# Attention times v for two heads at once into four common PSUM banks, float64 weights converted in pairs of blocks, and a table of shifted due times

## The chip, the cores and the metric

The kernel runs on one core of a Trainium2 chip. Its metric is the time of one execution on the device in microseconds; the median of three runs stands for a kernel. A profile is one further execution, with its own time.

## The reference

Three parts follow one another, on 4 batches, 8 heads, 576 positions and heads of 64 (2304 tokens of width 512):

```
scores = q @ k^T / 8                       # per batch and head, 576 x 576
mask   = scores >= 32nd largest of its row
attn   = softmax(scores where mask, else -1e9)
x = (attn @ v), heads side by side         # 2304 x 512
h = x @ w_in;  g = h * sigmoid(1.702 h);  x = g @ w_out     # 512 -> 2048 -> 512
a = x @ w1;  b = x @ w2;  out = ((a * b) @ w3) @ w_out2     # 512 -> 1024 -> 1024 -> 512
```

q, k and v are float32. The six weight matrices come as float64 (37.7 MB in all). In the kernel moe2's w_out is called w4.

## The kernel before, in words

**Tiles.** The 2304 tokens are 18 tiles of 128. For each tile the kernel runs eight heads (`head`), then `tile_end` (the attention output is scaled and split), then `moe` (both feed-forward parts). A number that must be more exact than float16 is held as a high and a low float16 half, so each product of 512 x 512 x 128 is four blocks of three matmuls, 12 in all (`product_op`, lines 532 to 534). A tile needs 168 such matmuls: four products `h` with w_in, four steps of `x2` with w_out, two each of `a` and `b` with w1 and w2, and two steps of `o` with w34, which is w3 times w4, worked out once.

**A head.** `S` (line 760) writes the scores into one of two double PSUM banks. VectorE finds the 32nd largest by four MAX8 and three MATCH_REPLACE8 (lines 782 and 785). ScalarE cuts, takes the exponential and makes the high half (lines 800, 803, 809), GpSimd the low half (812, 813). A DMA transpose of SyncE's queue (`f_t`, line 816) brings both into one of the two buffers `ats`. Nine matmuls (`f_av`, line 823) multiply by v. The sums of two heads lie side by side in the one PSUM bank `av_ps`; ScalarE copies one half of them into `xsb` (`x0`, line 863) and VectorE adds the other (`x1`, line 867). The products have three PSUM banks of their own (`mm`).

**The weights.** `load64` turns a float64 block of 128 x 512 into float32 without reading it as a number: a load into a raw buffer (line 372), then `w low` (ScalarE, line 377), `w sign` (ScalarE line 387 or GpSimd line 382), `w main` (ScalarE, line 391) and `w join` (VectorE, line 395), which frees the raw buffer. The 72 blocks go through in the order w4, w3, w_in, w_out, w1 and w2. Raw buffers are borrowed: eight in the place of w12 for w4 and w3 (`raw_c`), four in the place of wout for w_in and w_out (`raw_b`), and two for w1 and w2 (`raw_t`), one of which is the tile `psb` and one a part of `tsb`. Each converted block adds to a Gram matrix (line 422), from which its matrix's scale comes; then an fp32 matmul by the identity (line 459) and two instructions (lines 462 and 465) split it into halves. Where one matrix's float32 blocks lie, the next matrix's halves are put later, so the matrices follow each other.

**The order.** Nothing is scheduled by the compiler. `Order.run` simulates the five engines (T for TensorE, V, A, G and D for SyncE's DMA queue) with a cost per operation, takes for each free engine the ready operation with the smallest due time, hands out buffers of the pools, and emits the instructions in that order, in which each engine then runs them. Due times come from `head_due` (9 us apart for the first 16 heads, then 5.7), from `conv_due` (2 us for each weight block) and offsets in the code. Where an operation can go to two engines, the second has an extra wait, as `SIGN_G` for the sign on GpSimd.

Of the kernel before, what the change touches and what calls it, by code (L numbers as in the profile page):

```python
# [35 lines left out]
class Order:  # L36
# [22 lines left out]
    def op(self, alts, due, deps=(), env=None, acq=(), rel=(), tag="", lat=None):  # L59
        o = Op()  # L60
        o.alts, o.prio, o.lat = alts, due, lat
        o.acq = [(a, env, a) if isinstance(a, str) else a for a in acq]
        o.rel = [(a, env, a) if isinstance(a, str) else a for a in rel]
        o.left, o.users, o.ready, o.end, o.why = 0, [], 0.0, None, None
        o.tag, o.seq, o.done = tag, len(self.ops), False
        for d in deps:
            if d is not None:
                d.users.append(o)
                o.left += 1
        self.ops.append(o)  # L70
        return o
# [98 lines left out]
SIGN_G = 0.5  # L170
# [7 lines left out]
def kernel(  # L178
# [56 lines left out]
    def raws(w, n, first=0):  # L235
        return [w[:, (first + 2 * i) * C : (first + 2 * i + 2) * C] for i in range(n)]
# [9 lines left out]
    tsb = mem([P, 7, C], F32, "tsb")  # L246
    hsb = mem([P, 3, 2 * C], F16, "hsb")
    fsb = mem([P, 3, C], F32, "fsb")
    psb = mem([P, 2, C], F32, "psb")
# [12 lines left out]
    av_ps = ps.tile([P, C], F32, tag="av", name="av")  # L262
    m_ps = [ps.tile([P, C], F32, tag=f"mm{i}", name=f"mm{i}") for i in range(3)]
# [32 lines left out]
    od.pool("av", [av_ps[:, 0 : 2 * VW].rearrange("p (j w) -> p j w", j=2)])  # L296
# [67 lines left out]
    def load64(dst, src, raw_pool, deps):  # L364

        E = {}
        due = conv_due()

        def f_load():
            nc.sync.dma_start(E[raw_pool].bitcast(U32), src.bitcast(U32))
# [28 lines left out]
        sg = op([("A", 0.63, f_sign_a, 0.0), ("G", 0.75, f_sign, SIGN_G)], due, deps=[lo], tag="w sign")  # L401
        mn = act(0.57, due, f_main, deps=[ld, sg], tag="w main")
        return dve(0.65, due, od.two(f_join), deps=[sg, mn], env=E, rel=[raw_pool], tag="w join")
# [112 lines left out]
    def rows(w, i, j):  # L516
        return w[i * P : (i + 1) * P, j * C : (j + 1) * C]
# [27 lines left out]
    def weights():  # L545
        c4 = [load64(block(wout, i), w4[i * P : (i + 1) * P, :], "raw_c", []) for i in range(8)]
        c3 = [load64(block(win, 2 * f + kc), rows(w3, f, kc), "raw_c", []) for f in range(8) for kc in range(2)]
# [8 lines left out]
        cin = [load64(block(w12, 4 * j + i), rows(w_in, i, j), "raw_b", c3 + sp4) for j in range(NG) for i in range(KB)]  # L556
# [3 lines left out]
        for f in range(8):  # L560
# [35 lines left out]
        cout = [  # L596
            load64(block(w12, i), w_out[i * P : (i + 1) * P, :], "raw_b", cin + [ready["win"][i]]) for i in range(16)
        ]
        io, so, do = l2_scale([block(w12, i) for i in range(16)], cout)
        ready["wout"] = split_all(wout, 0, [block(w12, i) for i in range(16)], so, [do] + cout + pr, "wout")  # L600
        srcs = [rows(w, i, j) for w in (w1, w2) for j in range(NP_) for i in range(KB)]
        c12 = [load64(block(w12, i), srcs[i], "raw_t", [ready["wout"][i]]) for i in range(16)]
# [142 lines left out]

    def head(t, h, X):
# [70 lines left out]

        def f_av():
            for b, s0, r, n in pt:
                v2 = vhold[b, hp]["v2"]  # L820
                for i in range(9):
                    blk = i if i < 5 else i - 5
                    nc.tensor.matmul(  # L823
                        X["av", hp][r : r + n, j], E["at"][:, i, r : r + n], v2[:, j, blk, :], start=(i == 0), stop=(i == 8)
                    )
# [6 lines left out]
        s = pe(0.5 if len(pt) == 1 else 0.65, due - 1000 - 8, f_s, deps=qready[t] + kd, env=E, acq=["sp"], rel=rel, tag="S")  # L832
# [8 lines left out]
        for i in range(3):  # L841
# [11 lines left out]
        rel = [("v2", vhold[b, hp], "v2") for b, _, _, _ in pt if j == 1 and t == tiles_of[b][-1]]  # L853
        av = pe(
            0.55 if len(pt) == 1 else 0.75, due - 1000 + 10, f_av, deps=[tr] + vd + [X["av op", h - 1] if j else None],
            acq=[] if j else [("av", X, ("av", hp))], rel=[("at", E, "at")] + rel, tag="av",
        )
        X["S", h] = s
        X["av op", h] = av
        if j == 1:  # L860

            def f_x0():
                nc.scalar.copy(X["x"][:, 2 * hp : 2 * hp + 2, :], X["av", hp][:, :, D : P + 1])

            def f_x1():
                xs = X["x"][:, 2 * hp : 2 * hp + 2, 0:D]
                nc.vector.tensor_tensor(xs, xs, X["av", hp][:, :, 0:D], op=ALU.add)

            x0 = act(0.17, due + 12, f_x0, deps=[X["av op", h - 1], av, X.get("x0")], env=X, acq=["x"] if hp == 0 else [], tag="x0")
            X["x0"] = X["x0p", hp] = x0  # L870
            X["x1", hp] = dve(0.2, due - 40, f_x1, deps=[x0], env=X, rel=[("av", X, ("av", hp))], tag="x1")
# [68 lines left out]
    def moe(t, X):  # L940
# [8 lines left out]
        gs = []  # L949
        for j in range(NG):  # L950
# [3 lines left out]
                [X["xt"]] + ready["win"][4 * j : 4 * j + 4], [("mm", E, "mm")], [("t", X, "t")] if j == NG - 1 else [], "h",  # L954
# [20 lines left out]
            a = act(0.58, due, f_th, deps=[pr, ths], env=E, acq=["f"], tag="tanh")  # L975
            a = act(0.53, due, f_th1, deps=[a], tag="th1")
# [46 lines left out]
        ps_, pd = [], []  # L1023
        for j in range(NP_):
# [3 lines left out]
                [x2t] + ready["w12"][4 * j : 4 * j + 4], [("mm", Ea, "mm")], [], "a",  # L1028
# [120 lines left out]
```

## Time and profile before

| | |
|---|---|
| median of three runs | 1120.21 us (1118.58 to 1121.06) |
| the profiled execution | 1122.92 us, of which its span is 1121.1 us |
| busy in it: TensorE, VectorE, ScalarE, GpSimd | 987.4, 938.6, 833.6, 755.6 us |
| DMA packets' share of 16 engines | 67.6% on SyncE's queue |

The span goes from the first to the last instruction. Busy time is the union of an engine's instructions, so overlapping matmuls count once, and a stretch that is busy all through still can hold fewer matmuls than it might. A wait row names the instruction that stood still and the one that released it.

### The profile page before, as it was taken

The numbers are of one execution on the slowest core, as the hardware profiler recorded it, in microseconds if no ns is written. First come the engines' busy times: TensorE is split into PE (matmuls) and PEld (weight loads), VectorE is DVE, ScalarE is ACT, GpSimd is POOL, SyncE is SP. The second block draws the span as 40 slices with busy tenths as digits, with TensorE's granted clock in tenths as the row PEclk, the third lists the DMA queues.
The fourth block names the chain that finished last, engine by engine and source line by source line (L and its number), as shares of the span: only waits on it lengthen the run. The fifth ranks groups of instructions, "written<-read, shape, count | busy, mean of one in ns | idle before, by whom it ended". The sixth has DMA issues, their size and how long they took to land.

```text
span 1121.1 us, 18684 instructions
## 1 busy us (share of the span) xinstructions
PE 987.4 (88%) x5798; PEld 504.9 (45%) x5798; DVE 938.6 (84%) x2079; ACT 833.6 (74%) x1589; POOL 755.6 (67%) x1092
## 2 busy tenths in 40 slices
PE   1367898688879999999999998999999999999995
PEld 1233343344434445555445454454445555455442
DVE  4798899699799999989999878998998999997311
ACT  6987858988978776878788687777777777777421
POOL 6733332555547886989798887878879796776320
PEclk9998999879989999999999999999999999999998
DMA  7969958768746675786776859576865664746331
GB/s 236 293 151 229 257 101 221 197 138 177 160 113 110 128 132 118 127 167 115 136 143 122 155 103 156 107 131 124 134 140 97 135 136 94 144 83 122 76 57 38
DMA packets 428740, 156.96 MB, mean 140 GB/s; under 512 B 406624, under 2 KB 414816, under 8 KB 428640
## 3 DMA queue, kind: packets, MB, share of 16 engines
q1 hardware_dynamic: 428640, 155.78, 67.6%
q8 instruction: 45, 0.74, 0.3%
q14 instruction: 55, 0.45, 0.1%
HBM read 52.43 MB, written 4.72 MB: 51 GB/s over the span
## 4 chain that ended last, share of the span: by engine, by line
PE 38%; DVE 16%; DMA 14%; ACT 12%; POOL 12%; issue 7%; SPq 1%; POOLq 0%; ACTq 0%; DVEq 0%
PE mm L532 10%; PE mm L534 10%; PE mm L533 10%; DVE m8s L782 7%; DVE wsb L785 6%; DMA ats<-hlb 5%; DMA tsb<-hsb 5%; PE av L823 4%; PE s_ps L760 3%; POOL hsb L343 2%; POOL hlb L813 2%; ACT ysb L803 2%; POOL hsb L935 1%; ACT s_ps L800 1%; PE mm L459 1%
## 5 line engine op out<-in xcount | busy, mean ns | idle before, releaser
L782 DVE MAX8 m8s<-wsb 128x8 f32<-128x576 f32 x432 | 323.6, 755 | 5.3
L785 DVE MATCH_REPLACE8 wsb<-m8s,wsb 128x576 f32<-128x576 f32 x288 | 213.8, 743 | 0.0
L532 PE MATMUL mm<-w,tsb 128*128 128x512 f16 x432 | 164.5, 381 | 12.8 <-DMA tsb<-hsb 10.2
L532 PEld LDWEIGHTS <-tsb 128*128 128x128 f16 x1072 | 105.2, 98 | 136.9 <-DMA tsb<-hsb 28.3
L813 POOL TENSOR_TENSOR hlb<-ysb,hlb 128x512 f16<-128x512 f32 x144 | 166.7, 1158 | 0.0
L534 PE MATMUL mm<-w,tsb 128*128 128x512 f16 x432 | 164.2, 380 | 0.0
L533 PE MATMUL mm<-w,tsb 128*128 128x512 f16 x432 | 164.2, 380 | 0.0
L534 PEld LDWEIGHTS <-tsb 128*128 128x128 f16 x1072 | 105.4, 98 | 128.8 <-issue 4.0
L533 PEld LDWEIGHTS <-tsb 128*128 128x128 f16 x1072 | 105.4, 98 | 116.0 <-issue 17.1
L532 PE MATMUL mm<-wout,tsb 128*128 128x512 f16 x352 | 134.0, 381 | 7.9 <-DMA tsb<-hsb 4.0
L782 DVE MAX8 m8s<-s_ps 128x8 f32<-128x576 f32 x144 | 109.1, 757 | 34.6 <-PE s_ps L760 29.6
L800 ACT ACTIVATE s_ps<-s_ps,m8s 128x576 f32<-128x576 f32 x144 | 102.5, 712 | 44.6 <-DVE m8s L782 36.8
L534 PE MATMUL mm<-wout,tsb 128*128 128x512 f16 x352 | 133.9, 380 | 0.0
L533 PE MATMUL mm<-wout,tsb 128*128 128x512 f16 x352 | 133.9, 380 | 0.0
L803 ACT ACTIVATE ysb<-s_ps,nbs,asm 128x576 f32<-128x576 f32 x144 | 119.7, 831 | 16.9 <-DVE nbs L792 10.6
L823 PE MATMUL av<-v2s,ats 128*128 128x130 f16 (+1 forms) x1440 | 105.7, 224 | 20.2 <-DMA ats<-hlb 17.1
L532 PE MATMUL mm<-win,tsb 128*128 128x512 f16 x288 | 111.6, 388 | 9.8 <-DMA tsb<-hsb 6.2
L760 PE MATMUL s_ps<-kts,qts 128*128 128x288 f16 (+1 forms) x640 | 101.0, 298 | 18.6 <-ACT ysb L803 15.4
L823 PEld LDWEIGHTS <-ats 128*128 128x128 f16 (+1 forms) x1440 | 90.2, 102 | 57.7 <-DMA ats<-hlb 29.6
L970 POOL TENSOR_TENSOR fsb<-fsb 128x512 f32<-128x512 f32 x68 | 87.0, 1279 | 38.1 <-ACT fsb L961 37.0
L533 PE MATMUL mm<-win,tsb 128*128 128x512 f16 x288 | 111.2, 386 | 0.0
L534 PE MATMUL mm<-win,tsb 128*128 128x512 f16 x288 | 111.2, 386 | 0.0
(182 smaller groups left out, 1877.8 us busy)
## 6 DMA issues: line engine op xcount, KB each, us to landing
w<-in_moe_w_dram SPq DMA_DIRECT2D x16, 512.0 KB, 6.8
wout<-in_moe_w_in_dram SPq DMA_DIRECT2D x16, 512.0 KB, 5.2
wout<-in_moe_w_out_dram SPq DMA_DIRECT2D x16, 512.0 KB, 4.5
qts<-qts SPq DMA_DIRECT2D x36, 128.0 KB, 2.4
out_dram<-fsb SPq DMA_DIRECT2D x18, 256.0 KB, 2.5
w<-in_moe_w_out_dram SPq DMA_DIRECT2D x8, 512.0 KB, 4.6
psb<-in_moe_w_dram SPq DMA_DIRECT2D x8, 512.0 KB, 4.8
tsb<-in_moe_w_dram SPq DMA_DIRECT2D x8, 512.0 KB, 5.6
```

Source lines behind the costliest of these rows:

```text
L343: nc.gpsimd.tensor_tensor(lo(), src(), hi(), op=ALU.subtract)
L532: nc.tensor.matmul(o, a[:, i, :], hi, start=(first and i == 0), stop=False)
L533: nc.tensor.matmul(o, a[:, i, :], lo, start=False, stop=False)
L534: nc.tensor.matmul(o, a[:, 4 + i, :], hi, start=False, stop=(last and i == 3))
L760: nc.tensor.matmul(E["sp"][r : r + n, i], qe[q_][:, h, r : r + n], kt[:, j, i * HS : (i + 1) * HS], start=k_ == 0, stop=k_ == 1,)
L782: nc.vector.max(out=E["m8"][:, 8 * i : 8 * i + 8], in_=E["sp"] if i == 0 else E["w"])
L785: nc.vector.match_replace(out=two(E["w"]) if i == 0 else E["w"], in_to_replace=E["m8"][:, 8 * i : 8 * i + 8], in_values=E["sp"] if i == 0 ...
L800: nc.scalar.activation(E["sp"], E["sp"], AF.Prelu, bias=E["m8"][:, TOPK - 1 : TOPK], scale=-1.0, alpha=1.0 / FAR)
L803: nc.scalar.activation(two(E["y"]), E["sp"], AF.Exp, bias=E["nb"], scale=nesc)
L813: nc.gpsimd.tensor_tensor(hl()[:, S + SR : 2 * S], E["y"][:, 0:SM], hl()[:, 0:SM], op=ALU.subtract)
L823: nc.tensor.matmul(X["av", hp][r : r + n, j], E["at"][:, i, r : r + n], v2[:, j, blk, :], start=(i == 0), stop=(i == 8))
L970: nc.gpsimd.tensor_tensor(E["f"], E["f"], E["f2"], op=ALU.mult)
```

## The change

Attention times v is issued once for two heads, when both transposes have landed, into any one of four common `mm` banks, and both `ats` buffers come free after it. A conversion takes two blocks: a load of 1 MB, and each of the four operations over 1024 columns, with half as many raw buffers of twice the size; `raw_t` becomes one. `psb` and `tsb` become one tile. Some operations get an order among themselves (`S` after `S`, products `h`, `a` and `b` in turn, `he` after `tanh`). Every due time is shifted by an amount from a table by kind of operation and time (`LATER`, 83 kinds by 8 times), some engine choices by `LONGER`, and `SIGN_G` is 0. The diff, cut to its core:

```
-        o.alts, o.prio, o.lat = alts, due, lat
+        o.alts, o.prio, o.lat = [(e, c, f, max(w + LONGER.get((tag, e), 0.0), -1.0) if len(alts) > 1 else w) for e, c, f, w in alts], due + later(tag, due), lat
...
-SIGN_G = 0.5
+SIGN_G = 0.0
+TIMES = (-20, 60, 130, 220, 330, 500, 750, 1000)
+LATER = {
+    'S': (22, -25.5, -29.5, -19.5, -7, -8.5, -11, -16),
+    'a T': (7, 2.5, 26, 10.5, 13.5, 38, 9, 6),
+    'av': (-30, -25.5, -16, 15, 24.5, 40, 19, -0.5),
+    'gram': (7.5, 4.5, 14, 56.5, 72.5, 72.5, 69.5, 86.5),
+    'w load': (0, 3.5, -18, -0.5, 30.5, 49, -1, 2),
+    'w sign': (-1.5, 6, 0, -23, -23.5, -13.5, -12.5, -13.5),
...
+}
+LONGER = {
+    ('g hi', 'V'): 2, ('g lo', 'V'): -5.5, ('g lo', 'G'): -1.5, ('kv hi', 'V'): 7, ('kv lo', 'V'): -3.5,
...
+}
+def later(tag, due):
+    v = LATER.get(tag)
+    if v is None:
+        return 0.0
+    x = min(max(due + 1000 if due < -500 else due, TIMES[0]), TIMES[-1])
+    j = max(i for i in range(len(TIMES) - 1) if TIMES[i] <= x)
+    w = (x - TIMES[j]) / (TIMES[j + 1] - TIMES[j])
+    return v[j] * (1 - w) + v[j + 1] * w
...
-        return [w[:, (first + 2 * i) * C : (first + 2 * i + 2) * C] for i in range(n)]
+        return [w[:, (first + 4 * i) * C : (first + 4 * i + 4) * C] for i in range(n)]
...
+    tpsb = mem([P, 9, C], F32, "tpsb")
+    tsb, psb = tpsb[:, 0:7], tpsb[:, 7:9]
...
-    av_ps = ps.tile([P, C], F32, tag="av", name="av")
-    m_ps = [ps.tile([P, C], F32, tag=f"mm{i}", name=f"mm{i}") for i in range(3)]
+    m_ps = [ps.tile([P, C], F32, tag=f"mm{i}", name=f"mm{i}") for i in range(4)]
...
-        ld = dma(1.3, due - 20, f_load, deps=deps, env=E, acq=[raw_pool], tag="w load", lat=3.6)
-        lo = act(0.65, due, f_low, deps=[ld], tag="w low")
+        ld = dma(1.3, due - 20, f_load, deps=deps, env=E, acq=[raw_pool], tag="w load", lat=1.8 + 1.8 * n)
+        lo = act(0.2 + 0.44 * n, due, f_low, deps=[ld], tag="w low")
...
+    def load_pairs(w, first, srcs, raw_pool, deps):
+        res = []
+        for i, src in enumerate(srcs):
+            k_ = first + 2 * i
+            res += [load64(w[:, k_ * C : (k_ + 2) * C], src.bitcast(U32), raw_pool, deps(i))] * 2
+        return res
...
-    od.pool("raw_c", raws(w12, 8))
-    od.pool("raw_b", raws(wout, 4))
-    od.pool("raw_t", [tsb[:, 5:7, :].rearrange("p a b -> p (a b)"), psb.rearrange("p a b -> p (a b)")])
+    od.pool("raw_c", raws(w12, 4))
+    od.pool("raw_b", raws(wout, 2))
+    od.pool("raw_t", [tpsb[:, 5:9, :].rearrange("p a b -> p (a b)")])
...
         def f_av():
-            for b, s0, r, n in pt:
...
+            for j_, e in enumerate((X["E", h - 1], E)):
+                for b, s0, r, n in pt:
...
-        av = pe(
-            0.55 if len(pt) == 1 else 0.75, due - 1000 + 10, f_av, deps=[tr] + vd + [X["av op", h - 1] if j else None],
-            acq=[] if j else [("av", X, ("av", hp))], rel=[("at", E, "at")] + rel, tag="av",
-        )
...
         if j == 1:
+            av = pe(
+                1.06 if len(pt) == 1 else 1.4, due - 1000 + 10, f_av, deps=[X["tr", h - 1], tr, last_of.get("av")] + vd,
+                acq=[("mm", X, ("av", hp))], rel=[("at", X["E", h - 1], "at"), ("at", E, "at")] + rel, tag="av",
+            )
...
-                he = act(0.48, due, f_he, deps=[pr], env=E, acq=[("f", E, "f2")], rel=["mm"], tag="he")
+                he = act(0.48, due, f_he, deps=[pr, ta], env=E, acq=[("f", E, "f2")], rel=["mm"], tag="he")
```

## Rows read from the trace of the kernel before

**Rows 1.** The page's first two parts: busy time of each engine, and the busy share of the span's 40 slices in tenths (28 us each), with TensorE's granted clock.

```profile
span 1121.1 us, 18684 instructions
PE 987.4 (88%) x5798; PEld 504.9 (45%) x5798; DVE 938.6 (84%) x2079; ACT 833.6 (74%) x1589; POOL 755.6 (67%) x1092
PE   1367898688879999999999998999999999999995
...
DVE  4798899699799999989999878998998999997311
ACT  6987858988978776878788687777777777777421
...
PEclk9998999879989999999999999999999999999998
```

**Rows 2.** Busy time by stretch, over three stretches: to the last split of a weight, from there to the end of the heads, and the rest. Columns: stretch, its length, busy time (and instructions) of TensorE's matmuls, its weight loads, VectorE, ScalarE and GpSimd, then the granted clock, the DMA engines' share and GB/s.

```profile
0.00:345.00 345.00, 245.53 (x1294) 124.10 (x1295) 287.38 (x599) 286.19 (x523) 172.11 (x255) 0.94 0.79 187
345.00:1035.00 690.00, 667.78 (x4165) 347.69 (x4164) 634.30 (x1445) 522.13 (x1018) 564.62 (x813) 1.00 0.68 127
1035.00:1122.00 87.00, 74.08 (x342) 33.09 (x340) 16.93 (x36) 25.27 (x49) 18.87 (x26) 0.95 0.28 58
```

**Rows 3.** TensorE's instructions in order of time, the end of the weights' splits, a single head's attention times v between products, two heads' back to back, and a piece of the last stretch. Columns: start, time, line and operation, count.

```profile
343.01 2.14 PE L459 MATMUL mm<-w,ident 128*128 128x512 f32 x4
...
701.76 0.68 PE L823 MATMUL av<-v2s,ats 128*128 128x130 f16 x9
702.28 0.38 PE L532 MATMUL mm<-w,tsb 128*128 128x512 f16 x1
...
489.69 1.21 PE L823 MATMUL av<-v2s,ats 128*128 128x130 f16 x18
490.74 0.38 PE L532 MATMUL mm<-win,tsb 128*128 128x512 f16 x1
...
1050.03 0.38 PE L534 MATMUL mm<-wout,tsb 128*128 128x512 f16 x1
1050.25 0.38 PE L532 MATMUL mm<-wout,tsb 128*128 128x512 f16 x1
```

**Rows 4.** What TensorE waited for, in all, how often and the longest: first in the stretch to 345 us, then from 345 us to the end.

```profile
PE s_ps L760 <- ACT ysb L803: 13.1, 7, 5.0
PE mm L422 <- DVE w L395: 12.7, 7, 3.9
PE av L823 <- DMA ats<-hlb: 12.1, 8, 3.1
PE mm L422 <- DVE wout L395: 9.0, 2, 4.9
PE mm L422 <- DVE win L395: 8.8, 5, 3.2
...
PE mm L532 <- DMA tsb<-hsb: 17.1, 13, 7.1
PE av L823 <- DMA ats<-hlb: 5.0, 7, 1.3
PE mm L532 <- ACT fsb L967: 2.6, 2, 1.3
```

**Rows 5.** The sign of the conversion, line 387 on ScalarE and line 382 on GpSimd, and two casts of ScalarE of different length, as groups by form: busy time, mean ns, idle time before.

```profile
L387 ACT ACTIVATE w<-wout 128x512 f16<-128x512 f32 x19 | 14.5, 778 | 0.0
L387 ACT ACTIVATE win<-w 128x512 f16<-128x512 f32 x11 | 8.3, 769 | 0.0
L387 ACT ACTIVATE w<-psb 128x512 f16<-128x512 f32 x7 | 5.4, 770 | 0.0
L387 ACT ACTIVATE wout<-w 128x512 f16<-128x512 f32 x5 | 3.8, 764 | 0.0
L387 ACT ACTIVATE w<-tsb 128x512 f16<-128x512 f32 x6 | 4.6, 774 | 0.0
L809 ACT CAST hlb<-ysb 128x576 f16<-128x576 f32 x144 | 97.1, 677 | 5.7 <-DMA ats<-hlb 4.4
L929 ACT CAST hsb<-fsb 128x512 f16<-128x512 f32 x68 | 42.0, 618 | 13.6 <-POOL fsb L970 11.7 <-DMA tsb<-hsb 1.6
```

**Rows 6.** The instructions on the tile `psb`, one of the two raw buffers of w1 and w2, from 230 to 330 us: line, engine, operation, count, shortest, median and longest in ns, first and last start.

```profile
L372 SPq DMA_DIRECT2D psb<-in_moe_w_dram x8: 333/528/635, 233.9 to 315.0; - x8
L377 ACT ACTIVATE w<-psb x8: 763/786/796, 241.1 to 320.1; 128x512 uint16<-128x512 uint8 x8
L391 ACT ACTIVATE psb<-psb x8: 645/656/680, 243.6 to 322.6; 128x512 f32<-128x512 f32 x8
L395 DVE SCALAR_TENSOR_TENSOR w<-psb,w x8: 674/936/1420, 244.4 to 323.3; 128x512 uint32<-128x512 uint32 x8
DMA to landing us min/median/max: 3.8/4.8/5.2
```

**Rows 7.** What SyncE's queue waited for from 345 to 1035 us, the largest rows and the one on attention times v.

```profile
SPq L816 <- POOL hsb L935: 43.8, 20, 4.7
SPq L1077 <- POOL psb L342: 36.2, 14, 7.8
SPq L1077 <- ACT hsb L329: 29.4, 8, 6.3
SPq L816 <- POOL hlb L813: 26.9, 22, 3.4
...
SPq L816 <- PE av L823: 11.5, 14, 2.4
```

More of the change, by code (lines that the diff above doesn't have):

```diff
@@ L368, in load64 @@
         E = {}
-        due = conv_due()
+        n = dst.shape[1] // C
+        due = 0.0
+        for _ in range(n):
+            due = conv_due()
         def f_load():
-            nc.sync.dma_start(E[raw_pool].bitcast(U32), src.bitcast(U32))
+            raw = E[raw_pool].bitcast(U32)
+            nc.sync.dma_start(raw if n == 1 else raw.rearrange("p (n c) -> p n c", n=n), src)
         def f_low():
@@ L397, in f_join @@
             )
-        ld = dma(1.3, due - 20, f_load, deps=deps, env=E, acq=[raw_pool], tag="w load", lat=3.6)
-        lo = act(0.65, due, f_low, deps=[ld], tag="w low")
-        sg = op([("A", 0.63, f_sign_a, 0.0), ("G", 0.75, f_sign, SIGN_G)], due, deps=[lo], tag="w sign")
-        mn = act(0.57, due, f_main, deps=[ld, sg], tag="w main")
-        return dve(0.65, due, od.two(f_join), deps=[sg, mn], env=E, rel=[raw_pool], tag="w join")
+        ld = dma(1.3, due - 20, f_load, deps=deps, env=E, acq=[raw_pool], tag="w load", lat=1.8 + 1.8 * n)
+        lo = act(0.2 + 0.44 * n, due, f_low, deps=[ld], tag="w low")
+        sg = op([("A", 0.19 + 0.44 * n, f_sign_a, 0.0), ("G", 0.2 + 0.55 * n, f_sign, SIGN_G)], due, deps=[lo], tag="w sign")
+        mn = act(0.13 + 0.44 * n, due, f_main, deps=[ld, sg], tag="w main")
+        return dve(0.08 + 0.57 * n, due, od.two(f_join), deps=[sg, mn], env=E, rel=[raw_pool], tag="w join")
+    def load_pairs(w, first, srcs, raw_pool, deps):
[4 more added lines that the diff above has]
+        return res
     ncol = [0]
@@ L545, in weights @@
     def weights():
-        c4 = [load64(block(wout, i), w4[i * P : (i + 1) * P, :], "raw_c", []) for i in range(8)]
-        c3 = [load64(block(win, 2 * f + kc), rows(w3, f, kc), "raw_c", []) for f in range(8) for kc in range(2)]
+        c4 = load_pairs(wout, 0, [rows(w4, i, 0) for i in range(4)], "raw_c", lambda i: [])
+        across = [w3[f * P : (f + 1) * P, :].rearrange("p (n c) -> p n c", n=2) for f in range(8)]
+        c3 = load_pairs(win, 0, across, "raw_c", lambda i: [])
         i4, s4, d4 = l2_scale([block(wout, i) for i in range(8)], c4)
@@ L555, in weights @@
         )
-        cin = [load64(block(w12, 4 * j + i), rows(w_in, i, j), "raw_b", c3 + sp4) for j in range(NG) for i in range(KB)]
+        cin = load_pairs(w12, 0, [rows(w_in, i, j) for j in range(NG) for i in range(KB // 2)], "raw_b", lambda i: c3 + sp4)
         sp3, pr = [], []
@@ L595, in weights @@
         ready["win"] = split_all(win, 0, [block(w12, i) for i in range(16)], si, [di] + sp3, "win")
-        cout = [
-            load64(block(w12, i), w_out[i * P : (i + 1) * P, :], "raw_b", cin + [ready["win"][i]]) for i in range(16)
-        ]
+        cout = load_pairs(w12, 0, [rows(w_out, i, 0) for i in range(8)], "raw_b", lambda i: cin + ready["win"][2 * i : 2 * i + 2])
         io, so, do = l2_scale([block(w12, i) for i in range(16)], cout)
         ready["wout"] = split_all(wout, 0, [block(w12, i) for i in range(16)], so, [do] + cout + pr, "wout")
-        srcs = [rows(w, i, j) for w in (w1, w2) for j in range(NP_) for i in range(KB)]
-        c12 = [load64(block(w12, i), srcs[i], "raw_t", [ready["wout"][i]]) for i in range(16)]
+        srcs = [rows(w, i, j) for w in (w1, w2) for j in range(NP_) for i in range(KB // 2)]
+        c12 = load_pairs(w12, 0, srcs, "raw_t", lambda i: ready["wout"][2 * i : 2 * i + 2])
         ready["c12"] = c12
@@ L816, in f_t, with heads_av @@
             nc.sync.dma_start_transpose(out=E["at"], in_=hl())
+        def heads_av():
+            return X["av", hp][:, 0 : 2 * VW].rearrange("p (j w) -> p j w", j=2)
         def f_av():
-            for b, s0, r, n in pt:
[L820 to L824, printed above, removed]
-                    )
+            for j_, e in enumerate((X["E", h - 1], E)):
+                for b, s0, r, n in pt:
+                    v2 = vhold[b, hp]["v2"]
+                    for i in range(9):
+                        blk = i if i < 5 else i - 5
+                        nc.tensor.matmul(
+                            heads_av()[r : r + n, j_], e["at"][:, i, r : r + n], v2[:, j_, blk, :], start=(i == 0), stop=(i == 8)
+                        )
         kd = [d for b, _, _, _ in pt for d in kready[b, hp]]
@@ L949, in moe @@
         gs = []
+        pr = None
         for j in range(NG):
@@ L973, in f_t @@
                 nc.sync.dma_start_transpose(out=E["t"], in_=E["h"])
-            a = act(0.58, due, f_th, deps=[pr, ths], env=E, acq=["f"], tag="tanh")
-            a = act(0.53, due, f_th1, deps=[a], tag="th1")
+            ta = act(0.58, due, f_th, deps=[pr, ths], env=E, acq=["f"], tag="tanh")
+            a = act(0.53, due, f_th1, deps=[ta], tag="th1")
             if tail or (t * NG + j) % 8 < G_DVE:
@@ L1027, in moe @@
                 due + 5 * j, lambda Ea=Ea: Ea["mm"], lambda: x2e["x2t"], w12, [4 * j + i for i in range(4)], True, True,
-                [x2t] + ready["w12"][4 * j : 4 * j + 4], [("mm", Ea, "mm")], [], "a",
+                [x2t, pb] + ready["w12"][4 * j : 4 * j + 4], [("mm", Ea, "mm")], [], "a",
             )
```

38 lines of the change are left out of this document (24 added, 14 removed), and 71 rows, old and new, of tables (LATER, LONGER).

## Prediction

> **What bounds the kernel now.** I read the page's slices first. TensorE is busy 88% of the span, but not evenly: its slices stand at 6 to 9 up to about the thirteenth and at 9 from there on, while VectorE's stand at 8 and 9 nearly throughout [rows 1]. So there are stretches with different limits, and I cut the span in three. The first cut is at 345 us, where the last split of a weight ends [rows 3]; the second at 1035 us, where VectorE's work on heads ends. In the middle stretch TensorE is busy 667.78 of 690 us (97%) and VectorE 634.30 (92%): the reader should see TensorE as the bound there, with 22 us to be had at most by that measure. In the last stretch TensorE works off what is left, 74 of 87 us. In the first it is busy 245.53 of 345 us, idle 99 us, while ScalarE (286.19, 83%) and VectorE (287.38, 83%) are the busiest [rows 2].
>
> A busy TensorE isn't a TensorE that could do no more, so I check with starts. In the last stretch matmuls of 512 columns are marked 0.38 us long but start 0.22 us apart (1050.03, 1050.25), and a head's nine small ones take 702.28 - 701.76 = 0.52 us up to the next product's start [rows 3]. From 1035 us on the matmuls are dense, so the work there can't shrink by order. The consequence for the whole: after 345 us the end is TensorE's work that is left plus small stalls, so a change pays mostly through the first stretch, by having the weights ready earlier.
>
> Third, the waits. Before 345 us TensorE waits for conversions (line 422 behind the joins of line 395: 12.7 + 9.0 + 8.8 = 30.5 us), for score banks (13.1) and for the heads' transposes (12.1). After it, of its 22 + 13 idle microseconds 17.1 are for products' transposes (7.1 of them one wait), 5.0 for heads' transposes and 2.6 for a bank that ScalarE still reads (line 967) [rows 4].
>
> **The change, part by part.** *Attention times v for two heads.* Eighteen matmuls at a time. Two such groups back to back took 490.74 - 489.69 = 1.05 us, against 2 x 0.52 = 1.04 for two single ones [rows 3]. So by the nearest row the pairing gains 0, and I take that. The bound for a gain: a single group is marked 0.68 us, 0.16 more than its place; were that tail saved once for each of 72 pairs, it were 12 us. Bound for a loss: 0, for the matmuls stay the same.
>
> *Four common banks.* A bank for v was private; now a product can have it whenever no pair is in it. The only wait for a bank after 345 us that the trace shows is 2.6 us [rows 4], since an order made for three banks avoids the others. I take -5 for banks and order together in the middle stretch: about a quarter of its 22 us. Bounds: -12 (half) and +10.
>
> *Both `ats` buffers are held until the pair is done.* A third transpose must wait for the pair. One before already waited for the product at times: 11.5 us in 14 waits, 2.4 the longest [rows 7]. Between pairs of heads lie 12.3 us in the middle stretch (112 heads remain after the 32 whose work starts in the first 345 us: 690 / 112 = 6.2 each); I estimate the time needed from a landing to the freed pair at 1.05 us plus a queue of a few products, so I cost it at nothing. Its cover is that slack; without it, see the rivals.
>
> *Half as many conversions.* Of the 72 signs 48 are on ScalarE [rows 5], so it issues 36 + 36 + 24 = 96 fewer instructions (low, main, sign). The fixed part of one, from two casts: 677 ns for 576 columns and 618 for 512, so 0.92 ns a column and 618 - 472 = 146 ns that don't shrink [rows 5]. 96 x 0.146 = 14.0 us off ScalarE's 286.19: 272.2. VectorE saves 36 fixed parts, no more than a few microseconds; it isn't the sole bound there, so 0. SyncE issues 36 loads fewer of 0.53 us each [rows 6], some 19 us, on a queue whose waits are far longer; 0 too, as these waits cover it. SIGN_G at 0 can move signs from ScalarE to GpSimd, which has most of its time free before 345 us (172 of 345 busy [rows 2]); no gain or loss taken.
>
> A page bears on the fixed part: the Trainium skill, VectorE: DVE Perf Modes, section "The TRN2 errata", says that a ScalarE instruction with its source in SBUF pays 224 cycles at 1.2 GHz whatever its length, which is 187 ns; rows 5 give 146. By the page the saving would be an estimated 17.9 us instead of 14.0, and the sum some 4 us lower.
>
> *Fewer, larger raw buffers.* This speaks against the change. For w1 and w2 two raw buffers become one. Before, `psb` was loaded eight times between 233.9 and 315.0 us, one cycle in 81.1 / 7 = 11.6 us, and the other buffer goes in step with it, so two blocks take 11.6 us. Such a cycle is a load of 4.8 us, four operations of 0.786 + 0.770 + 0.656 + 0.936 = 3.15 us, and 3.65 us of waiting [rows 5, 6]. After: the load of 1 MB between 4.8 and 9.6 us, taken at 5.8, since the two loads before also shared the DMA engines; the operations 2 x 3.15 - 4 x 0.146 = 5.7; the waiting taken at half, 1.8, as part of it was for the other buffer's turn on the same engines, bounds 0.5 and 3.65. That is 13.3 us, +1.7, and over seven cycles +12 us. Bounds: 11.0 (-4 in all) and 19.0 (+52).
>
> *The tuned order.* Every due time moves, so every step may; what bounds the gain is the busiest engine of the first stretch. With ScalarE's 272.2 us at today's share, 83%, it would last 328 us; at VectorE's share of the middle stretch, 92%, 296 us. I take 88%, half-way: 309 us, -36. That is the largest choice in this working. With the raw buffers' +12 the first stretch is 24 us shorter, 321 us. Bounds: -53 (92%, and -4) and +35 (83%, and +52). In the middle stretch VectorE must keep up: its 921.7 us before 1035 would have to fit in about 1006, a share of 92%, as high as it reached there [rows 2]. The last stretch stays: 0.
>
> *Sum.* -5 - 36 + 12 = -29 us. The profiled execution took 1122.92 us (span 1121.1): 1093.9. The median of the runs shown is 2.7 below the profiled one, so 1091.
>
> **The rivals.** *One raw buffer sets the first stretch* (slower). Place: w1 and w2, from 234 to 345 us. If the load takes 9.6 and the waits stay, +52 instead of +12, and the sum is +11: 1131; if the order also only reaches 83%, -17 instead of -36, about 1150. It decides from a cycle of 11.6 + (5 + 36) / 7 = 17.5 us on. For it: the order is fixed by modelled costs, the chip adds waits, and with one buffer nothing covers a late load. Against it: TensorE can do products h and x2 of the first tiles meanwhile, and the other buffer's work no longer stands in between. For the load's price there is also a figure: the Trainium skill, DMA: Bandwidth & Descriptors, section "Bandwidth", gives 6.15 us of DMA time for 1 MB from HBM. By that the sum would be an estimated 2 us higher than with my 5.8; no trace of before has such a load.
>
> *The order gains nothing on the chip.* The transposes, not the due times, hold TensorE up, and the first stretch stays at ScalarE's 83%: 328 us, but with +12 again: -17 + 12 = -5, or 1115. For it: the waits for transposes and for loads don't shorten by a new order. Against: 30.5 us of TensorE's waits are for joins, which an order can bring forward.
>
> *The order gains more.* The first stretch at 92%, the cycle of the raw buffer unchanged, 12 us of the middle stretch and some 10 of the last (13 idle): -49 - 12 - 10 = -71, 1049; halfway between this and the forecast 1070. Against it: VectorE would need a share of 95% and more before its end.
>
> *The pair holds up SyncE's queue.* If each of the 56 pairs in the middle stretch stopped it for the 2.4 us seen at worst, that is 134 us of queue; the four largest waits there sum to 136 us [rows 7] beside TensorE's 22 us of idle time, so about 22 us would reach the end: 1113.
>
> **How the numbers follow.** The forecast, 1075 to 1105 us, has 0.43; the larger gain, below 1075, 0.19; nothing gained or the queue held up, 1105 to 1122, 0.18, of which 0.05 lies within 0.2% of before; the raw buffer and other new waits, above 1122, 0.20. A difference under 0.2%, about 2 us, can't be told from none here. So faster 0.75, same 0.05, slower 0.20. The predicted time is 1091. The range of 8 in 10 is 1057 to 1128: it leaves out the far part of the larger gain (0.08) and of the raw-buffer rival (0.12).
>
> **What would show it.** Right: the last matmul of line 459 near 320 us instead of 345; ScalarE's share before it near 88%; loads of w1 and w2 some 13 us apart; TensorE still at 97% from there, and the groups of line 823 at about 1.05 us for 18. Wrong on the raw buffer: loads 17 us or more apart and waits of line 422 above 30 us. Wrong on the order: the first stretch near 335 us. Wrong on the buffers `ats`: waits of the queue at line 816 for line 823 far above 11.5 us, and waits of TensorE for products' transposes above 17 us. The prediction fails altogether if VectorE doesn't keep up, when the heads end after 1020 us and TensorE idles before the last tile.

## The result, and where the time went

The changed kernel takes 1086.81 us (median, 1085.55 to 1087.44) against 1120.63 for before, measured beside it. The ratio is 0.9703, with a 95% interval of 0.9676 to 0.9729: 3.0% faster, 33.8 us. I had forecast 1091. The profiled execution took 1085.55 us.

Its span is 1083.4 us. First the same stretches as in [rows 2], busy time by engine, same columns:

```profile
0.00:345.00 345.00, 252.26 (x1428) 135.77 (x1430) 294.47 (x608) 280.36 (x445) 204.03 (x284) 0.91 0.79 196
345.00:1035.00 690.00, 683.88 (x4214) 357.27 (x4212) 622.66 (x1424) 525.49 (x1022) 560.51 (x797) 1.00 0.67 126
1035.00:1122.00 87.00, 37.32 (x161) 15.96 (x159) 6.75 (x14) 10.22 (x20) 7.42 (x11) 0.95 0.11 24
```

In the first 345 us TensorE is busy 7 us longer than before; in the next 690 us it is busy 16 us longer and now idle 6 of them. So the larger part of the gain is not where the prediction had it. Nor does the clock bring it: the granted clock of the first stretch is 0.91, against 0.94 before.

Busy time hides overlap, so for the rest of this document I count TensorE's work by starts: each matmul at the step from start to start in a dense run (0.2157 us for 512 columns, 0.1225 for 288, 0.058 for attention times v, 0.44 for half an fp32 block, 0.057 for a Gram piece). This is 942 to 943 us in every kernel here, since all issue the same matmuls. What a stretch has beyond its work is lost time: waits, and matmuls at a lower granted clock. It is good to some 2 us. In microseconds:

```
                                     lost to 400   400 to 950   rest   span of profile
before                                   137           25        16        1121.1
changed                                  124            1        15        1083.4
```

The spans differ by 37.7 us, the lost times by 13 + 24 + 1 = 38. That they agree proves nothing, as the lost time is the span less the same work; what the table adds is where the time was lost.

TensorE's waits from 345 us to the end answer to the second part of [rows 4]. Columns: what waited for what, us in all, times, longest.

```profile
PE mm L650 <- DMA tpsb<-hsb: 9.0, 5, 6.7
PE s_ps L879 <- ACT ysb L922: 3.2, 3, 1.6
PE mm L650 <- ACT fsb L1092: 0.8, 1, 0.8
```

Of the 9.0 us for products' transposes 6.7 are one wait; it was 17.1 us in 13 waits before. The heads' transposes don't appear any more, and the waits for a product's bank are down from 2.6 to 0.8.

The raw buffer of w1 and w2, now one for a pair of blocks, answers to [rows 6] (line, engine, operation, count, shortest, median, longest ns, first and last start):

```profile
L481 SPq DMA_DIRECT2D tpsb<-in_moe_w_dram x8: 368/380/585, 236.1 to 334.9; - x8
L486 ACT ACTIVATE w<-tpsb x8: 1349/1368/1392, 247.8 to 341.5; 128x1024 uint16<-128x1024 uint8 x8
L500 ACT ACTIVATE tpsb<-tpsb x8: 1132/1152/1179, 251.1 to 344.7; 128x1024 f32<-128x1024 f32 x8
L504 DVE SCALAR_TENSOR_TENSOR w<-tpsb,w x8: 1205/1226/2516, 252.6 to 346.7; 128x1024 uint32<-128x1024 uint32 x8
```

One cycle is (334.9 - 236.1) / 7 = 14.1 us, where two blocks took 11.6 before. The weights therefore end later, not earlier: the last matmuls of the splits stand here, and at 343 us in [rows 3].

```profile
363.17 3.70 PE L576 MATMUL mm<-w,ident 128*128 128x512 f32 x8
```

Yet by 345 us TensorE and VectorE had done more of other work. Groups by form in the first 345 us, the first MAX8 of a head and the first matmul line of the products, of the changed kernel:

```profile
L650 PE MATMUL mm<-wout,tpsb 128*128 128x512 f16 x112 | 44.6, 398 | 9.2 <-DMA tpsb<-hsb 8.3 <-DVE w L709 0.6 <-DVE hsb L582 0.4
L901 DVE MAX8 m8s<-s_ps 128x8 f32<-128x576 f32 x37 | 28.0, 756 | 6.8 <-PE s_ps L879 5.9 <-ACT hlb L928 0.7 <-ACT hsb L1053 0.2
L650 PE MATMUL mm<-win,tpsb 128*128 128x512 f16 x48 | 18.2, 379 | 0.0
L650 PE MATMUL mm<-w,tpsb 128*128 128x512 f16 x4 | 1.5, 379 | 0.0
```

and of before:

```profile
L532 PE MATMUL mm<-wout,tsb 128*128 128x512 f16 x96 | 36.9, 384 | 7.2 <-DMA tsb<-hsb 3.3 <-DVE w L590 1.8 <-ACT fsb L967 1.1
L782 DVE MAX8 m8s<-s_ps 128x8 f32<-128x576 f32 x32 | 24.2, 757 | 8.6 <-PE s_ps L760 8.5
L532 PE MATMUL mm<-win,tsb 128*128 128x512 f16 x40 | 16.4, 409 | 3.1 <-ACT fsb L967 2.0 <-DVE win L465 0.6 <-DVE hsb L1005 0.5
L532 PE MATMUL mm<-w,tsb 128*128 128x512 f16 x8 | 3.0, 379 | 0.0
```

So 164 against 144 on the first of three product lines, 60 matmuls more or 13 us of work, and 37 heads begun against 32.

### The profile page after: what moved, and what is told of

The parts are those of the page before. It is cut to its first block, busy times and chain, and to the rows that moved or that the text cites. A ratio compares the mean times of both kernels' runs of the same rounds, so it can differ in the third digit from the quotient of the medians.

```text
span 1083.4 us, 18424 instructions
## 1 busy us (share of the span) xinstructions
PE 973.5 (90%) x5798; PEld 509.0 (47%) x5798; DVE 923.9 (85%) x2045; ACT 816.1 (75%) x1485; POOL 772.0 (71%) x1091
## 4 chain that ended last, share of the span: by engine, by line
PE 52%; DVE 13%; ACT 12%; DMA 9%; POOL 6%; issue 5%; SPq 0%; DVEq 0%; ACTq 0%; POOLq 0%
PE mm L650 14%; PE mm L651 13%; PE mm L652 13%; DVE m8s L901 5%; PE mm L946 4%; DVE wsb L904 4%; PE s_ps L879 4%; DMA tpsb<-hsb 3%; PE mm L576 3%; DMA ats<-hlb 3%; DMA wout<-in_moe_w_in_dram 1%; POOL hlb L932 1%; ACT ysb L922 1%; ACT w L486 1%; DVE w L504 1%
## 5 line engine op out<-in xcount | busy, mean ns | idle before, releaser
L650 PE MATMUL mm<-w,tpsb 128*128 128x512 f16 x432 | 164.9, 382 | 8.5 <-DMA tpsb<-hsb 8.5
L650 PEld LDWEIGHTS <-tpsb 128*128 128x128 f16 x1072 | 105.3, 98 | 137.1 <-DMA tpsb<-hsb 23.3
L652 PEld LDWEIGHTS <-tpsb 128*128 128x128 f16 x1072 | 105.5, 98 | 128.5 <-issue 3.5
L651 PE MATMUL mm<-w,tpsb 128*128 128x512 f16 x432 | 164.7, 381 | 0.0
L652 PE MATMUL mm<-w,tpsb 128*128 128x512 f16 x432 | 164.5, 381 | 0.0
L651 PEld LDWEIGHTS <-tpsb 128*128 128x128 f16 x1072 | 105.5, 98 | 112.9 <-issue 8.4
L650 PE MATMUL mm<-wout,tpsb 128*128 128x512 f16 x352 | 135.6, 385 | 9.8 <-DMA tpsb<-hsb 8.8
L651 PE MATMUL mm<-wout,tpsb 128*128 128x512 f16 x352 | 135.4, 385 | 0.0
L652 PE MATMUL mm<-wout,tpsb 128*128 128x512 f16 x352 | 135.2, 384 | 0.0
L650 PE MATMUL mm<-win,tpsb 128*128 128x512 f16 x288 | 109.2, 379 | 1.1 <-ACT fsb L1092 0.8
L652 PE MATMUL mm<-win,tpsb 128*128 128x512 f16 x288 | 109.1, 379 | 0.0
L946 PE MATMUL mm<-v2s,ats 128*128 128x130 f16 (+1 forms) x1440 | 96.7, 226 | 13.9 <-DMA ats<-hlb 12.8
L651 PE MATMUL mm<-win,tpsb 128*128 128x512 f16 x288 | 109.1, 379 | 0.0
L904 DVE MATCH_REPLACE8 wsb<-m8s,s_ps 128x576 f32<-128x576 f32 x144 | 107.7, 748 | 0.0
```

What stands on the lines that cost most here:

```text
L650: nc.tensor.matmul(o, a[:, i, :], hi, start=(first and i == 0), stop=False)
L651: nc.tensor.matmul(o, a[:, i, :], lo, start=False, stop=False)
L652: nc.tensor.matmul(o, a[:, 4 + i, :], hi, start=False, stop=(last and i == 3))
L904: nc.vector.match_replace(out=two(E["w"]) if i == 0 else E["w"], in_to_replace=E["m8"][:, 8 * i : 8 * i + 8], in_values=E["sp"] if i == 0 ...
L946: nc.tensor.matmul(heads_av()[r : r + n, j_], e["at"][:, i, r : r + n], v2[:, j_, blk, :], start=(i == 0), stop=(i == 8))
```

## The experiments

My theory from the two traces: the order carries the gain, by giving TensorE other work while the weights are late, and the two structural parts are worth little by themselves. The rival: the structure carries it (less ScalarE time, a fourth bank). A third question was my own slow rival: does the single raw buffer's cycle reach the end?

**The table away.** The changed kernel's structure with the old due times.

```
-            LONGER.get((tag, e), 0.0)
+            0.0
...
-SIGN_G = 0.0
+SIGN_G = 0.5
...
 def later(tag, due):
+    return 0.0
```

> The changed kernel without the table: later() returns 0, no extra waits from LONGER, SIGN_G back at 0.5. Pairs of blocks, attention times v for two heads and the four common banks stay. Theory 1 (the order carries the gain, the two structural parts are worth little by themselves): 1110 to 1130 us, near before's 1120. Theory 2 (the structure carries it: 14 us less of ScalarE and the fourth bank): 1085 to 1100 us. My prediction's sum without its order term of -36 would be 1120 + 12 - 5 = 1127.

Measured: 1107.92 us, ratio 0.9893 (0.9856 to 0.9930). Between the two theories: 11 us faster than before, 21 slower than the changed kernel.

**The structure away, the table kept.** Single blocks, attention times v head by head, three banks and one.

```
+    av_ps = ps.tile([P, C], F32, tag="av", name="av")
+    m_ps = [ps.tile([P, C], F32, tag=f"mm{i}", name=f"mm{i}") for i in range(3)]
...
+            res += [load64(block(w, k_ + m), src[:, m, :].bitcast(U32), raw_pool, deps(i)) for m in range(2)]
...
+    od.pool("raw_c", raws(w12, 8))
+    od.pool("raw_b", raws(wout, 4))
```

> The changed kernel with both structural parts undone: single blocks with eight, four and two raw buffers, attention times v head by head into a bank of its own, three banks for the products. The table, LONGER, SIGN_G = 0 and the added order of S, h, a, b and he stay. Theory 1 (order): 1085 to 1105 us; the table was made for other operations, so some of its gain is lost. Theory 2 (structure): 1115 to 1125 us. If the table only fits the one plan it was made for: above 1120.

Measured: 1116.04 us, ratio 0.9970 (0.9944 to 0.9996). This is the range of the second theory (1115 to 1125), but it doesn't show that theory: the table here shifts other operations than those it was made for, and on them it brings next to nothing.

**Only the attention times v undone.** Table and pairs of blocks stay; the diff is the first two lines above, with `f_av` and its wait for one head.

> The changed kernel with attention times v head by head into its own bank and three banks for the products; pairs of blocks and the table stay. If the fourth common bank matters, TensorE waits again for banks and transposes in the middle stretch: 1095 to 1110 us. If not, 1083 to 1092 us, and SyncE's queue waits less for attention times v than the 37 us of the changed kernel.

Measured: 1128.66 us, ratio 1.0080 (1.0058 to 1.0103): outside both of my ranges, slower than before. SyncE's queue did wait less for attention times v, 12.2 us from 345 to 1035 us. The profile shows that the loss isn't the banks' in the middle stretch (5 us lost there): to 400 us it loses 165. So this plan, too, is simply another plan. That raised the question of the next run.

**A control: the table in whole microseconds.**

```
+    v = [float(int(y)) for y in v]
     return v[j] * (1 - w) + v[j + 1] * w
```

> A control: the changed kernel with every entry of LATER cut to whole microseconds, a shift of at most 0.5 us for any operation, everything else the same. It says how much a time moves when the planner's choices are nudged. If the order is robust: 1083 to 1092 us. If each plan is a lucky draw: anything from 1085 to 1115 us, and then differences of that size between the other kernels prove nothing about their parts.

Measured: 1121.34 us, ratio 1.0025 (0.9999 to 1.0051). That is beyond even the wider range. Shifts of at most half a microsecond in due times take the whole gain away. TensorE's order is the same for its first 600 matmuls or so and differs from there. The waits from 345 us on come back:

```profile
PE mm L651 <- DMA tpsb<-hsb: 17.9, 9, 6.7
PE s_ps L880 <- ACT ysb L923: 6.1, 5, 3.7
PE mm L577 <- DVE w L583: 3.1, 1, 3.1
```

This settles how the first three runs must be read: whoever changes an operation gets another plan, and plans differ by more than the parts do. So I nudged the others as well, and then left the order alone.

**The table, nudged otherwise.** A fixed pseudo-random shift for each kind of operation.

```
+def nudge(tag):
+    return 0.5 * (zlib.crc32(b"a" + tag.encode()) / 2.0 ** 31 - 1.0)
...
-due + later(tag, due), lat
+due + later(tag, due) + nudge(tag), lat
```

> The changed kernel with its table, each kind of operation shifted by a fixed pseudo-random amount between -0.5 and 0.5 us. The rounded table took 1121.3 us where the exact one took 1086.8. If the table's gain belongs to one exact plan, this one too falls back to 1100 to 1125 us. If the rounded one was an unlucky draw, 1085 to 1095 us.

Measured: 1114.09 us, ratio 0.9939 (0.9924 to 0.9953): in the range for a gain that belongs to one exact plan.

**No table, nudged twice.** The same shifts, with `b"a"` and `b"b"`, on the kernel of the first experiment.

> The changed kernel without the table (as in the first experiment, 1107.9 us), each kind of operation shifted by a fixed pseudo-random amount between -0.5 and 0.5 us. If the 11 us of the structure are its own, 1100 to 1115 us. If they are luck of one plan, near 1120 or beyond in this run or in its sister with other shifts.

> The same with other pseudo-random shifts. Structure's own gain: 1100 to 1115 us. The two sisters and the first experiment together give the spread of a plan without a table.

Measured: 1123.02 (ratio 1.0031, 1.0016 to 1.0045) and 1094.08 us (0.9760, 0.9742 to 0.9779): one as a lucky plan would have it, the other better than either range. With the 1107.92 of the first experiment, one structure gives a spread of 29 us. Its mean, 1108.3, is 12 us under before, but three such draws against one plan of before show nothing.

**The same order, each conversion in two halves.** Order and buffers are those of the changed kernel; only the instructions and loads are cut in two. The diff shows one of the four operations; the sign, `w main`, `w join` and the load are halved in the same way, on whichever engine they run.

```
-            nc.scalar.activation(low, b3, AF.Copy, scale=1.0 / 32, bias=-15.5 / 32)
+            for m in range(n):
+                i = slice(m * C, (m + 1) * C)
+                nc.scalar.activation(low[:, i], b3[:, i], AF.Copy, scale=1.0 / 32, bias=-15.5 / 32)
...
```

> The changed kernel in exactly its own order with the same buffers, but each of the four conversion instructions and the load of a pair is issued as two, of 512 columns and 512 KB each, one behind the other. It takes away only the larger instructions. My prediction priced them at 14.0 us of ScalarE's time and let them shorten the first stretch almost one for one: then 1099 to 1104 us. If the first stretch is not set by ScalarE's time but by waits between engines, 1086 to 1092 us.

Measured: 1093.10 us, ratio 0.9760 (0.9733 to 0.9786), 6 us above the changed kernel, with intervals that just don't touch, and between my two ranges. So larger instructions and loads together are worth about 6 us; the run doesn't part ScalarE's share from VectorE's, GpSimd's and the loads'. On ScalarE a sign's duration over a pair and over halves can be compared, here in the changed kernel and in this one:

```profile
L496 ACT ACTIVATE w<-wout 128x1024 f16<-128x1024 f32 x5 | 6.8, 1366 | 0.0
```

```profile
L503 ACT ACTIVATE w<-wout 128x512 f16<-128x512 f32 x10 | 7.0, 770 | 0.0
```

By durations a pair saves 2 x 770 - 1366 = 174 ns. But durations of neighbours overlap: ten halves of 770 ns are busy 7.0 us and not 7.7, hardly more than the 6.8 of five whole ones. The busy lines of the two pages, the changed kernel's first, show what ScalarE really loses:

```profile
PE 973.5 (90%) x5798; PEld 509.0 (47%) x5798; DVE 923.9 (85%) x2045; ACT 816.1 (75%) x1485; POOL 772.0 (71%) x1091
PE 975.3 (89%) x5798; PEld 508.3 (47%) x5798; DVE 928.2 (85%) x2081; ACT 822.2 (75%) x1571; POOL 775.7 (71%) x1113
```

ScalarE issues 1571 - 1485 = 86 instructions more, for 822.2 - 816.1 = 6.1 us more of its time: 0.07 us each.

**The same order, the loads of w1 and w2 twice.**

```
+            for _ in range(2 if raw_pool == "raw_t" else 1):
-            nc.sync.dma_start(raw if n == 1 else raw.rearrange("p (n c) -> p n c", n=n), src)
+                nc.sync.dma_start(raw if n == 1 else raw.rearrange("p (n c) -> p n c", n=n), src)
```

> The changed kernel in exactly its own order with the same buffers, but each of the eight loads of a pair of w1 and w2 is issued twice, one behind the other, into the same raw buffer (the second writes the same data). It lengthens the one raw buffer's cycle, 14.1 us, by the time of a second load, some 3 to 6 us. If that cycle sets the end, as my slow rival had it, seven cycles make 20 to 40 us and most of it reaches the end: 1105 to 1125 us. If TensorE has enough other work in its order by then, under 10 us: 1088 to 1097 us.

Measured: 1130.97 us, ratio 1.0104 (1.0063 to 1.0145), 44 us above the changed kernel and above both of my ranges. Two loads now stand for each pair, 16 in all:

```profile
L482 SPq DMA_DIRECT2D tpsb<-in_moe_w_dram x16: 367/373/585, 237.1 to 379.1; - x16
L487 ACT ACTIVATE w<-tpsb x8: 1342/1350/1369, 254.7 to 385.0; 128x1024 uint16<-128x1024 uint8 x8
```

The second load of a pair is not issued until the first has landed, and SyncE's queue stands still for that. The first and the last pair of loads in order of time (from the start of the first to the end of the second's issue), then the queue's wait for these landings and TensorE's waits for transposes, from 225 to 400 us:

```profile
237.13 6.40 SPq L482 DMA_DIRECT2D tpsb<-in_moe_w_dram  x2
373.19 6.24 SPq L482 DMA_DIRECT2D tpsb<-in_moe_w_dram  x2
...
SPq L482 <- DMA tpsb<-in_moe_w_dram: 42.0, 8, 5.6
PE mm L651 <- DMA tpsb<-hsb: 13.6, 3, 6.5
PE mm L947 <- DMA ats<-hlb: 10.6, 2, 6.4
```

The same waits for transposes in the changed kernel:

```profile
PE mm L650 <- DMA tpsb<-hsb: 3.1, 2, 1.8
PE mm L946 <- DMA ats<-hlb: 1.3, 1, 1.3
```

A cycle is (373.2 - 237.1) / 7 = 19.4 us, 5.3 longer, and the last pair's first operation starts 385.0 - 341.5 = 43.5 us later than in the changed kernel: as much as the end. So in this order time added to these loads reaches the end one for one. Through what, the run doesn't show: the raw buffer is free later, but the queue that also issues the transposes stood still for 42 us too, and TensorE's waits for transposes in these 175 us are 24.2 us, where the changed kernel has 4.4.

**A table chosen for plans that bear disturbance.** From the changed kernel's table, entries moved at random; kept when the plan, run through in its order with costs disturbed by some per cent and transfers delayed, ended earlier on the mean.

```
 LATER = {
-    'S': (22, -25.5, -29.5, -19.5, -7, -8.5, -11, -16),
...
```

> The changed kernel with another table: starting from its own, the entries of LATER and LONGER were moved at random, and kept where the plan, run through with each operation's modelled cost disturbed by some per cent and each transfer delayed by a random part of a microsecond, ended earlier on the mean. So it is a plan chosen to lose less when the chip departs from the planner's costs. If a plan's fate on the chip is mostly luck: 1087 to 1120 us, as with the nudged tables. If plans that bear disturbance also hold on the chip: 1070 to 1083 us.

Measured: 1078.94 us, ratio 0.9631 (0.9592 to 0.9670): the fastest kernel here, 8 us under the changed one, and in the range for plans that bear disturbance. It is one such plan. Its profile by stretch, columns as in [rows 2]:

```profile
0.00:345.00 345.00, 250.47 (x1407) 133.80 (x1407) 292.85 (x598) 275.42 (x437) 205.67 (x281) 0.92 0.79 195
345.00:1035.00 690.00, 682.49 (x4210) 357.19 (x4211) 616.69 (x1412) 530.40 (x1030) 570.71 (x821) 1.00 0.68 127
1035.00:1122.00 87.00, 39.55 (x183) 17.59 (x181) 4.64 (x11) 10.59 (x21) 9.81 (x13) 0.99 0.12 27
```

The first two stretches are much like the changed kernel's, with 7 us more lost in all by the count below; the gain is in the last, where 5 us are lost and not 15. There the changed kernel has one wait of 6.7 us for a product's transpose; from 950 us on this one has 1.6 us of such waits in all. The profiled spans, 1079.8 and 1083.4 us, differ by 3.6 us, the medians by 8.

**One structural part each, without the table.** The pieces are those shown above.

> The changed kernel without the table and with single blocks (eight, four and two raw buffers): only attention times v for two heads, the four common banks and the added order of S, h, a, b and he are left. Plans without a table differ by some 15 us from each other, so the time alone proves little; what is read is TensorE's lost time. Kernels with both parts and no table lose 7 to 10 us from 400 to 950 us, before loses 25. If the four banks are what empties that stretch: under 12 us there. If the pairs of blocks are: 18 us or more. Time 1095 to 1125 us.

> The changed kernel without the table, attention times v head by head into its own bank and three banks for the products: only the pairs of blocks and the added order are left. If the four banks empty the stretch from 400 to 950 us: 18 us lost or more there. If not: under 12 us. In the stretch to 400 us it shows the pairs by themselves: before loses 137 us there, the three kernels with both parts and no table 125 to 143. Time 1095 to 1130 us.

Measured: 1113.26 us (ratio 0.9945, 0.9923 to 0.9967) with attention times v for two heads and the four banks; 1124.88 (1.0041, 1.0017 to 1.0066) with the pairs of blocks. From 400 to 950 us they lose 29 and 18 us. By the first the pairs of blocks should be what empties that stretch, by the second the banks; so neither part alone does in these two plans, and which mixture does stays open. To 400 us the pairs alone lose 148 us, more than any of the three kernels with both parts. TensorE's lost time of all:

```
                                     lost to 400   400 to 950   rest   median us
before                                   137           25        16     1120.6
changed                                  124            1        15     1086.8
  same order, halves                     131            1        15     1093.1
  same order, w1 and w2 loaded twice     170           -1        16     1131.0
another table                            129            3         5     1078.9
table rounded                            137           14        23     1121.3
table nudged                             136           13        22     1114.1
no table                                 132            7        25     1107.9
no table, nudged a                       143           10        25     1123.0
no table, nudged b                       125            7        16     1094.1
no table, v for two heads only           124           29        17     1113.3
no table, pairs of blocks only           148           18        14     1124.9
table, v head by head                    165            5        16     1128.7
table, neither part                      138           13        23     1116.0
```

The column to 400 us spans 46 us, the middle one 30, the last 20. Single blocks under the table with the common banks were not tried.

One more number bears on luck. `Order.run` in each kernel also returns the end that the planner models, before any chip is involved. It is 1101.4 us for before and 1055.0 for the changed kernel, but 1080.5 for the rounded table and 1088.5 for the nudged one: 26 and 34 us lost, where 35 and 27 were measured. So shifts of half a microsecond spoil more than half of the table's gain in the planner's own account already. The table fits one plan, and losing that plan is not bad luck on the chip alone. The three plans without a table are modelled at 1089.4, 1087.9 and 1075.4 us, in the order of the list, and the other table at 1051.4. Yet the chip adds between 12 us (v for two heads only, modelled at 1101.0) and 44 us (table, v head by head, at 1084.5), so the model foretells the time only to some 30 us.

## Why the prediction was right, and where it was right by chance

**The direction and the size** came out: 1091 against 1086.8. The step that named TensorE's work as what is left after the weights, and its lost time as all that can be gained, holds: all kernels issue the same matmuls, and the gain is lost time. How that lost time would fall was mis-sized in two terms that partly made up for each other, so that 1091 lies so near is in part luck. Of the signs that I gave for being right, TensorE at 97% (it is 683.88 / 690 = 99%), loads about 13 us apart (14.1) and 1.05 us for eighteen matmuls came; the last split near 320 us and ScalarE near 88% did not. One reading of [rows 1] was loose: TensorE's first two slices stand at 1 and 3.

**The first stretch, -36 + 12 = -24: too much, and by a wrong picture.** The weights were to be ready earlier. I let ScalarE's share of the first stretch rise from 83% to 88% and the weights end at 321 us. ScalarE's share is 280.36 / 345 = 81%, and the splits end at 367 us. The failed step is the half-way choice of 88%: the order doesn't pack ScalarE, it fills TensorE's and VectorE's gaps with heads and products. The first stretch ends beyond the 335 us that I gave as the sign of being wrong on the order, and the lost time to 400 us still fell by 13 us.

**The middle stretch, -5: too little.** 25 us lost became 1. I priced a quarter of the waits away because the trace of before showed few waits for banks. The new plan took all of them, those for transposes first, though transposes landed no sooner: the medians of the two largest kinds are 3.2 and 3.4 us, and were 3.2 and 3.3. The exact table gets to 1; rounded or nudged it loses 14 and 13 there. Without any table three plans with both structural parts lose 7 to 10, so the table alone is not what empties this stretch.

**The raw buffer, +12: right in kind, low in size.** 14.1 us a cycle were measured, 13.3 forecast; seven cycles make 98.8 - 81.1 = 17.7 us more than before. The load of 1 MB landed in 6.0 us in the median (the page's list of DMA issues: count, KB each, median us to landing), near the 5.8 I had taken; what was low is mostly the waiting. The doubled loads show that time added to these loads counts fully in the end, as the slow rival said, though not whether by the buffer or by the queue; the rival's own price, 19 us a cycle, came only there.

```profile
tpsb<-in_moe_w_dram SPq DMA_DIRECT2D x8, 1024.0 KB, 6.0
```

The Trainium skill, DMA: Bandwidth & Descriptors, section "Bandwidth", has 6.15 us for 1 MB. The trace's 6.0 lies near it but is not the same measure: the page gives the DMA engines' busy time for loads that GpSimd issues, the trace the time from issue to landing for SyncE's. The changed kernel's other loads of 1 MB landed in 5.4 to 7.2 us in the median.

**ScalarE's fixed part, 14.0 us: too much, and from the wrong measure.** 146 ns from two casts was low as a duration: a pair's sign is 174 ns shorter than its halves in the same order, and 2 x 778 - 1366 = 190 against [rows 5]. The Trainium skill, VectorE: DVE Perf Modes, section "The TRN2 errata", gives 224 cycles at 1.2 GHz, which is 187 ns; as durations the trace's 174 and 190 agree with the page rather than with my two rows. As a price per instruction the page's figure is not borne out. In the run with halves 86 instructions cost ScalarE 6.1 us, 0.07 each, because neighbours overlap. I had checked this on TensorE, by starts, and not on ScalarE. The end moved by the same 6 us, less than half of what I took.

**Signs moved to GpSimd: nothing taken, and it took more off ScalarE.** ScalarE has 14 of the 36 signs, where it had 48 of 72; they take it 18.8 us, against the 36.6 of [rows 5], which is about as much as its whole busy time fell by (833.6 to 816.1):

```profile
L496 ACT ACTIVATE wout<-w 128x1024 f16<-128x1024 f32 x4 | 5.3, 1334 | 0.0
L496 ACT ACTIVATE w<-tpsb 128x1024 f16<-128x1024 f32 x3 | 4.0, 1345 | 0.0
L496 ACT ACTIVATE win<-w 128x1024 f16<-128x1024 f32 x2 | 2.7, 1361 | 0.0
```

These three groups and the one of 6.8 us above are all. What that is worth at the end, no run shows.

**Attention times v for two heads: 0, right.** Two heads' eighteen matmuls in the changed kernel take 711.56 - 710.52 = 1.04 us to the next product's start, as two singles took:

```profile
710.52 1.21 PE L946 MATMUL mm<-v2s,ats 128*128 128x130 f16 x18
711.56 0.38 PE L650 MATMUL mm<-wout,tpsb 128*128 128x512 f16 x1
```

**The two `ats` buffers: right that it costs nothing, though the sign showed.** SyncE's queue waits three times as long for attention times v, 35.9 us against the 11.5 of [rows 7], in the same 345 to 1035 us, and TensorE's waits for transposes fell all the same:

```profile
SPq L935 <- PE mm L946: 35.9, 20, 4.0
```

**The rivals.** Nothing gained by the order, 1115, is about what the nudged table (1114.1) and the rounded one (1121.3) took, but not the one on trial. The raw buffer's cycle stayed under the 17.5 us from which that rival decides, and the pair held up SyncE's queue for 35.9 us, not 134. What no rival said is that the order's value belongs to one exact plan.

## What to carry to other kernels

Where an order is written by a planner, an edit of one part changes the whole plan, and plans of the same parts lay 29 us apart here: judge a part by keeping the order and altering only that part, nudge the order before believing a gain of that size, and read the planner's own end beside the time. Price an instruction on any engine by what a run of them keeps it busy, not by its duration. Count the bounding engine's work by starts and its lost time by stretch; the lost time told at once which stretch paid. One plan chosen for bearing disturbed costs held on the chip and gained a further 8 us; that the choice did it is not shown by one plan.

## What the runs showed that I had not expected

A table whose entries were changed by at most 0.5 us lost 34.5 us, the whole gain. Loading the eight pairs of w1 and w2 twice stopped SyncE's queue for 42 us and moved the end by 44. Halving 36 conversions cost ScalarE 0.07 us an instruction, where durations say 0.17. And a kernel whose weights are ready 22 us later (the splits end at 367 and not 345 us) is 34 us faster.
